# Attention by pairs of heads: shared loads, products on column halves, and the first block turned on TensorE

## The chip, the cores and the metric

One core of one Trainium2 chip. The metric is device microseconds of one execution. The kernel before ran three times: 1150.33, 1153.37 and 1156.15 us, median 1153.37 us. A profile is one further execution, with its own time.

## What is computed

Sparse attention over 4 batches x 8 heads x 576 rows x 64 columns, then two MLPs on the 2304 x 512 result. Per row of scores, only what lies within tau of the row's maximum is kept.

```python
scores = scale * np.matmul(q, k.transpose(0, 1, 3, 2))
thresh = np.max(scores, axis=-1, keepdims=True) - tau
scores = np.where(scores >= thresh, scores, -1000000000.0)
attn = np.exp(scores - np.max(scores, axis=-1, keepdims=True))
attn = attn / (np.sum(attn, axis=-1, keepdims=True) + 1e-09)
x = np.matmul(attn, v)                       # heads side by side: 2304 x 512
h = x @ w_in                                 # 512 -> 2048
x = (np.maximum(h, 0) + alpha * np.minimum(h, 0)) @ w_out
h = x @ w2_in
out = (h - np.tanh(h)) @ w2_out
```

The weights come as 64-bit words and are made into float32 on the chip.

## The kernel before

The 2304 rows are nine blocks of 256: block 2b and 2b+1 are the first and second 256 rows of batch b, and block 8 is the last 64 rows of all four batches. Attention fills the blocks in this order, and layer 1 of the MLP takes each block when its eight heads are there; layer 2 follows.

**Attention.** A visit is one head and one block (64 visits, eight to a block). `prep` (L461) loads the queries (`rq`, one half of the rows on each half of the partitions), the keys (`ks`, the same 64 rows on both halves) and `v` (`vs`), and splits v into three bfloat16 planes (`rest`, L490, on VectorE or GpSimd). `attend` (L600) makes the scores of two tiles of 128 rows, in float32 (L609): the two tiles lie on the two row halves of the array. `softmax` (L512) then does for each tile: a row maximum on VectorE (L524), a threshold (L527), a Prelu and an Exp on ScalarE (L287 as called from L530, and L534), the inverse of the sum (L537, L540), the normalised rows as float16 (`upper`, L542, on ScalarE, VectorE or GpSimd), their remainder as float16 (`lower`, L552, VectorE), a copy of 64 columns (`mend`, L554), and a transposing DMA from SyncE's queue into `eT` (`turn`, L561; 144 of them). The products (L620 to L626) are nine matmuls with 128 stationary columns (two planes of v side by side) and five with 64 (the third plane, on alternating column halves, the last with 64 rows). `x_copy` and `x_add` (L633, L638) add the two halves of the output into `xt`, and each second visit `x_hi` and `x_lo` split it for the MLP. After each second visit of an odd block, `attend_left` (L667) does the last 64 rows of two heads as one tile, with products at L688 to L692.

**PSUM.** Three score tiles `sc` of two banks: visits of block 0 (`FRONT`, `SOLO` = 8) use all three, one tile per step; later the third is `acc` of the MLP. One bank each is left for `hp` and `pt`.

**MLP.** Float32r with a high and a low part: L763 makes h in 24 matmuls of 256 columns per pair of column blocks, L950 the output of layer 1, L872 and L879 that of layer 2. 32 pieces of layer-1 weights (`piece`, L359) are loaded (512 KB each) and split during attention.

**Order.** Nothing runs by a fixed loop: each step is given to `Plan` (L74) with its engines, costs, a rank and what it reads and writes; the planner simulates engines and picks, for each engine, the ready step of the lowest rank. Its order is then each engine's program. The ranks are those of the visit (`TA` per tile) plus an offset of the kind of step (`OFF`), with `PREP` for the loads of attention and `PA`, `PB` for the weight pieces. `BUFS` says how many buffers a kind of tile has: two of `eT`, each for one visit. 140 dummy steps of two matmuls (`N_WARM`, L994 to L1000) take the lowest rank on TensorE.

```python
    for _ in range(N_WARM):
        add({"PE": 0.236}, 1e9, warm, [("const", 2)], [("hp", 0)], [("hp", 0)])
```

Of the kernel before, what the change touches and what calls it, by code (L numbers as in the profile page):

```python
# [7 lines left out]

F32 = mybir.dt.float32
# [14 lines left out]
P = 128  # L24
# [35 lines left out]
XR = -995.8426  # L60
FLEX = 1
T_WARM = 0.3
N_WARM = 140
DVE_PEN = 0.6331
OFF = {"S": -2993.86, "M": -246.5, "TH": -1456.02, "E": -819.06, "X": -255.04, "R": -398.47, "N": -1092.63, "NL": -1335.92, "F": -898.27, "DT": -1391.78, "AV": 1778.6, "XC": -777.36, "XH": 1070.62}
# [3 lines left out]
    "rq": 2, "ql": 1, "ks": 3, "vs": 3, "v3": 3, "e": 3, "st": 2, "eT": 2, "xt": 1, "rw": 4, "raw0": 2, "raw1": 3, "tw": 2,  # L69
    "x0": 2, "x1": 2, "mr": 1, "pair": 1, "xl": 1, "g": GB, "gs": 1, "o": 2,  # L70
# [160 lines left out]
def attention_mlp_mlp(ctx: ExitStack, tc: tile.TileContext, kv, q0, q1, tau, w1i, w1o, alpha, w2i, w2o, out):  # L231
# [23 lines left out]
    none = cpool.tile([P, P], F32, name="none")  # L255
    qscale = cpool.tile([P, 1], F32, name="qscale")
# [8 lines left out]
    sc = [ppool.tile([P, 1024], F32, name=f"sc{k}") for k in range(3)]  # L265
    acc = [sc[2][:, t * 512:(t + 1) * 512] for t in range(2)]
# [52 lines left out]
    def turned_float(l, kind, qd, c, rank):  # L319
# [33 lines left out]
        add({"LOAD": P * 4096 / DMA_RATE}, rank, load, reads=[("products", NV - 1), ("products", -NV)] * l, writes=[raw, (*raw, 0)], takes=[("rw", raw), (f"raw{l}", raw)], lag=DMA_LAG)  # L353
# [104 lines left out]
    def ends(v):  # L458
        return visits[v][1] and visits[v][2] % 2 == 0

    def prep(v, rank):  # L461
        b, qb, h = visits[v]
        k = brings[v]
        rq, ql, ks, vs = ("rq", v), ("ql", v), ("ks", k), ("vs", k)
        head_now[b, h] = k
# [19 lines left out]
        def load_v(e):
            x = take(tpool, vs, [P, 5, 2, D], F32, "vs", BUFS["vs"])
            e.dma_start(out=x[:, :, 0], in_=kv[b, h][:, KW:].rearrange("p (c d) -> p c d", c=5))


        def rest(e, n):  # L490
            x = T[vs]
            out_ = x[:, :, 1] if not n else take(tpool, ("v3", k), [P, 5, D], BF16, "v3", BUFS["v3"])
            e.tensor_tensor(out=out_, in0=x[:, :, n], in1=x.bitcast(BF16)[:, :, n, 1::2], op=ALU.subtract)

        add({"LOAD": rate * P}, rank - 6, load_q, [ROOM], [rq], takes=[("rq", rq)], lag=DMA_LAG)
        if k == v:
            add({"LOAD": rate * KW}, rank - 6, load_k, [ROOM], [ks], takes=[("ks", ks)], lag=DMA_LAG)
            add({"LOAD": rate * VW}, rank - 6, load_v, [ROOM], [(*vs, 0)], takes=[("vs", vs)], lag=DMA_LAG)
        if ends(v):
            add({"LOAD": rate * D}, rank - 6, load_left, [ROOM], [ql], takes=[("ql", ql)], lag=DMA_LAG)  # L500
        for key in (rq, ql) if ends(v) else (rq,):
            add({"ACT": 0.25}, rank, lambda e, key=key: scale(e, key), [("const", 0), ROOM], [key])
# [6 lines left out]
    def banks_of(s):  # L509
        return [("acc", t) for t in range(2)] if s == 2 else [("sc", s, t) for t in range(2)]  # L510

    def softmax(tile, n, slots, rank, alone=False):  # L512
# [5 lines left out]
        eT = ("eT", tile)  # L518
# [22 lines left out]

        def upper(e, j):  # L542
# [29 lines left out]
        for j, s in enumerate(slots):  # L572
            both = banks_of(s)
# [3 lines left out]
            add({"ACT": 0.72}, rank + OFF["X"], lambda e, j=j: row_exp(e, j), [("const", 0), ROOM], [(*ej, 0), (*st, 2, j)])  # L577
# [3 lines left out]
        for j in js:  # L581
# [4 lines left out]
            add({"ACT": 0.18, "POOL": 0.2}, rank + OFF["F"], lambda e, j=j: mend(e, j), [(*fj, 1), ROOM], [(*fj, 2)])  # L586
            k = add({"SYNC": 1.4}, rank + OFF["DT"], lambda e, j=j: turn(e, j), [*[(*fj, n_) for n_ in range(3)], ROOM], [(*eT, j)],
                    takes=[] if j else [("eT", eT)], lag=2.0, after=[k] if j else [])
        return [(*eT, j) for j in js]

    def planes(k, c):
        return T["vs", k].rearrange("p c a d -> p c (a d)").bitcast(BF16)[:, c, 1::2]

    def third(k, c, rows=slice(0, P)):
        return T["v3", k][rows, c]

    def with_v(k):
        return [("vs", k, 0), ("vs", k, 1), ("v3", k)]

    def attend(v, rank):  # L600
        b, qb, h = visits[v]
        k = head_now[b, h]

        slots = [(2 * v + j) % 3 for j in range(2)] if v < FRONT else (0, 1)

        def scores(e, js):
            for c in CHUNKS:
                for j in js:
                    e.matmul(  # L609
                        sc[slots[j]][:, 192:192 + S][:, c], lhsT=T["rq", v][HALVES[j]], rhs=T["ks", k][HALVES[j], c], start=True, stop=True,  # L610
                    )

        alone = v < SOLO
        for js in ((0,), (1,)) if alone else ((0, 1),):
            add({"PE": 1.3}, rank + OFF["S"], lambda e, js=js: scores(e, js), [("ks", k), ("rq", v), ROOM], [("sc", slots[j], "s") for j in js],
                [b_ for j in js for b_ in banks_of(slots[j])])
        reads = softmax(v, 2, slots, rank, alone)
        pk, po, bank = out_of(v)

        def products(e):  # L620
            eT = T["eT", v]
            for n in range(9):
                e.matmul(po, lhsT=planes(k, n % 5 if n < 5 else n - 5), rhs=eT[:, n], start=(n == 0), stop=False, skip_group_check=True)  # L623
            for c in range(5):
                rows = slice(0, P) if c < 4 else HALVES[0]
                e.matmul(po[HALVES[c % 2]], lhsT=third(k, c, rows), rhs=eT[rows, c], start=False, stop=(c > 2), skip_group_check=True)  # L626

        add({"PE": 1.32}, rank + OFF["AV"], products, [*reads, *with_v(k), ROOM], [pk, ("products", v)], bank)
        m = 2 * b + qb
        xt = ("xt", v // 2)  # L630
        half = slice((h % 2) * D, (h % 2 + 1) * D)

        def x_copy(e):  # L633
# [352 lines left out]
    def clear(e):  # L986
        e.memset(none, 0.0)
# [126 lines left out]
```

## Time and profile before

| | |
|---|---|
| median of three runs | 1153.37 us |
| the profiled execution | 1156.52 us, of which its span 1154.7 us |
| TensorE busy | 1104.4 us (96%) |
| VectorE, ScalarE, GpSimd busy | 785.3, 661.2, 116.6 us |
| DMA | 123.13 MB, 107 GB/s over the span |
| mean granted TensorE clock | 0.984 |

The profiled execution is 3.15 us above the median of the runs; what is summed against the profile is corrected by that. In the profile PE is TensorE's matmuls, PEld its weight loads, DVE VectorE, ACT ScalarE, POOL GpSimd and SP SyncE, whose queue issues the DMAs. Matmuls overlap, so the mean of one (some 280 ns) is longer than the distance from one to the next; a timeline shows that distance.

### The profile page before, as it was taken

To read this page: it belongs to the slowest core of one execution; us is meant where nothing else is said; L and a number is where in the kernel's file an instruction comes from. 1 tells how busy PE (TensorE), PEld (TensorE's weight loads), DVE (VectorE), ACT (ScalarE), POOL (GpSimd) and SP (SyncE) were. 2 spreads that over 40 slices of the span, in tenths; PEclk is the share of its full clock that TensorE was granted. 3 is DMA by queue.
4 is the path that set the end of the run, shared out by engine and by line. 5 is a ranking of instruction groups with operands and counts; after the bars stand their busy time and mean duration, and the time that the engine had idled before them with its cause. 6 is when DMAs were issued, how large, how long until landed. Compare 5 with 4: busy or idle time off the path is not lost. (4 is left out here: it accounts for less than half of the span.)

```text
span 1154.7 us, 22609 instructions
## 1 busy us (share of the span) xinstructions
PE 1104.4 (96%) x8670; PEld 979.2 (85%) x8670; DVE 785.3 (68%) x1693; ACT 661.2 (57%) x1371; POOL 116.6 (10%) x125
## 2 busy tenths in 40 slices
PE   8888999999999999899999999999999999999998
PEld 5556777887787787778778999999999999999997
DVE  6788797776677667767766554998556556566554
ACT  5787788778777767677776343763323323323222
POOL 0112322101111101010010000000000000000000
PEclk8899899999999999999999999999999999999999
DMA  7989898747677556674657231641010010010000
GB/s 205 217 189 180 182 224 174 156 92 149 132 144 146 103 128 140 137 142 99 133 99 182 92 110 49 205 150 44 13 37 19 19 37 11 28 37 11 10 19 19
DMA packets 248588, 123.13 MB, mean 107 GB/s; under 512 B 219040, under 2 KB 227232, under 8 KB 248480
## 3 DMA queue, kind: packets, MB, share of 16 engines
q1 hardware_dynamic: 248480, 121.69, 46.1%
q8 instruction: 68, 1.11, 0.4%
q14 instruction: 40, 0.33, 0.1%
HBM read 69.21 MB, written 9.96 MB: 69 GB/s over the span
## 5 line engine op out<-in xcount | busy, mean ns | idle before, releaser
L763 PE MATMUL hp<-x,ihi 128*128 128x256 f32 x1728 | 324.5, 287 | 1.7 <-DVE st L537 1.3
L763 PEld LDWEIGHTS hp<-x,ihi 128*128 128x128 f32 x1728 | 269.7, 192 | 15.3 <-issue 8.8
L763 PE MATMUL hp<-x,ilo 128*128 128x256 f32 x864 | 244.9, 283 | 0.0
L950 PE MATMUL sc<-g,ohi 128*128 128x256 f32 x1152 | 216.8, 287 | 1.1 <-ACT o L282 0.8
L950 PEld LDWEIGHTS sc<-g,ohi 128*128 128x128 f32 x1152 | 178.8, 191 | 12.1 <-issue 8.7
L763 PEld LDWEIGHTS hp<-x,ilo 128*128 128x128 f32 x864 | 166.2, 192 | 0.0
L950 PE MATMUL sc<-g,olo 128*128 128x256 f32 x576 | 162.7, 283 | 0.0
L872 PE MATMUL sc<-wp,g 128*128 128x256 f32 x1134 | 144.9, 283 | 0.0
L872 PEld LDWEIGHTS sc<-wp,g 128*128 128x128 f32 x1134 | 140.0, 192 | 0.0
L552 DVE SCALAR_TENSOR_TENSOR rw<-e,st,rw 128x576 f16<-128x576 f32 x144 | 118.8, 846 | 13.7 <-ACT rw L282 11.6
L524 DVE TENSOR_REDUCE st<-sc 128x1 f32<-128x576 f32 x144 | 105.9, 748 | 12.3 <-PE sc L609 8.4
L287 ACT ACTIVATE e<-sc,st 128x576 f32<-128x576 f32 x144 | 103.0, 735 | 14.7 <-DVE st L527 11.7
L534 ACT ACTIVATE e<-e,natau 128x576 f32<-128x576 f32 x144 | 110.3, 769 | 0.2
L950 PEld LDWEIGHTS sc<-g,olo 128*128 128x128 f32 x576 | 110.3, 191 | 0.0
L282 ACT ACTIVATE rw<-e,st 128x576 f16<-128x576 f32 x116 | 86.8, 768 | 37.9 <-issue 17.4
L282 ACT ACTIVATE g<-mr 128x512 fp32r<-128x512 f32 (+1 forms) x126 | 73.7, 585 | 56.8 <-DVE mr L782 39.2
L623 PE MATMUL pt<-eT,vs 128*128 128x256 f16 x576 | 78.2, 284 | 29.0 <-DMA eT<-rw 23.5
L763 PE MATMUL pt<-x,ihi 128*128 128x256 f32 x576 | 105.2, 283 | 0.0
L784 DVE SCALAR_TENSOR_TENSOR mr<-mr,nalpha,hp 128x256 f32<-128x256 f32 x144 | 62.7, 476 | 58.2 <-ACT mr L777 57.6
L609 PE MATMUL sc<-ks,rq 64*128 64x320 f32 (+1 forms) x512 | 89.0, 437 | 8.0 <-ACT rq L282 4.7
L290 DVE TENSOR_TENSOR g<-mr,g 128x512 fp32r<-128x512 f32 (+1 forms) x132 | 85.4, 647 | 16.4 <-ACT g L282 15.2
L623 PEld LDWEIGHTS <-vs 128*128 128x128 bf16 x576 | 53.4, 101 | 48.0 <-issue 31.8
(96 smaller groups left out, 1530.0 us busy)
## 6 DMA issues: line engine op xcount, KB each, us to landing
ks<-in_kv_dram SPq DMA_DIRECT2D x56, 288.0 KB, 3.3
vs<-in_kv_dram SPq DMA_DIRECT2D x56, 160.0 KB, 3.0
rw<-in_w1i_dram SPq DMA_DIRECT2D x16, 512.0 KB, 5.2
rw<-in_w1o_dram SPq DMA_DIRECT2D x16, 512.0 KB, 4.2
rw<-in_w2i_dram SPq DMA_DIRECT2D x16, 512.0 KB, 4.9
rw<-in_w2o_dram SPq DMA_DIRECT2D x16, 512.0 KB, 4.1
x1d<-o SPq DMA_DIRECT2D x18, 256.0 KB, 2.4
rw<-x1d SPq DMA_DIRECT2D x9, 512.0 KB, 3.6
```

The lines of the kernel that those rows point to most:

```text
L282: e.activation(out=out_, in_=in_, func=AF.Copy, **({} if scale is None else {"scale": scale}))
L287: e.activation(out=out_, in_=in_, func=AF.Prelu, alpha=alpha, **kw)
L290: e.tensor_tensor(out=out_, in0=in_, in1=hi.bitcast(F32), op=ALU.subtract)
L524: e.tensor_reduce(out=T[st][:, 0, j:j + 1], in_=x(s), axis=AX.X, op=ALU.max, negate=True)
L534: e.activation(out=w_, in_=w_, func=AF.Exp, bias=natau, scale=1.0, accum_out=T[st][:, 2, j:j + 1])
L552: e.scalar_tensor_tensor(out=x_[:, S + D:], in0=w_, scalar=r, in1=x_[:, :S], op0=ALU.mult, op1=ALU.subtract)
L609: e.matmul(sc[slots[j]][:, 192:192 + S][:, c], lhsT=T["rq", v][HALVES[j]], rhs=T["ks", k][HALVES[j], c], start=True, stop=True,)
L623: e.matmul(po, lhsT=planes(k, n % 5 if n < 5 else n - 5), rhs=eT[:, n], start=(n == 0), stop=False, skip_group_check=True)
L763: e.matmul(hq[:, k, :], lhsT=weight(l, "i", part, f // 4)[:, c, (f % 4) * P:(f % 4 + 1) * P], rhs=T[f"x{x}", m][:, c, :], start=(n0 + n == ...
L784: e.scalar_tensor_tensor(out=T[r][:, k, :], in0=T[r][:, k, :], scalar=nalpha[:, f0 + k:f0 + k + 1], in1=hq[:, k, :], op0=ALU.mult, op1=ALU ...
L872: e.matmul(out_, lhsT=x[:, a], rhs=y[:, b], start=(n == 0 and i == 0 and number in (1, 2, 5, 4)), stop=(n == NPAIR - 1 and i == 2), skip_g ...
L950: e.matmul(acc[t][:, (c % 2) * BLK:(c % 2 + 1) * BLK], lhsT=w[:, c * P:(c + 1) * P], rhs=g[:, k, :], start=(f == 0 and n == 0 and c % 2 == ...
```

## The change

Two visits in a row are now the two 128-row halves of one pair of heads. A visit's two score tiles are the two heads (not two halves of the rows of one head), and queries, keys and v come once for both visits of a pair: `q` is one tile for two heads with 256 or 320 columns (the last 64 rows included, so `ql` is gone), `ks` holds one head on each half of the partitions. The products of a pair are made once, after its second visit: 23 terms (three planes), each of them two matmuls with 64 stationary columns, one head on each column half. The output is then already in the MLP's layout: `x_copy`, `x_add` and `xt` are gone, for the left rows `pair` and its sum as well.

In the first four pairs (`WHOLE` = 4: block 0) the normalised rows stay float32, are transposed by matmuls against an identity (`turn_whole`, `turn_last`), copied to `eT` (`bring`, `bring_last`), and multiplied with v in float32; there v isn't split, and pair 4, which shares its heads with pair 3, loads its v again. `sc` has two tiles everywhere, `acc` its own two banks, `SOLO` is 0; `eT` has three buffers of one head and 256 rows; 110 dummy steps; the planner's ranks are other ones.

```diff
-TA = 13.1642
-PA, PB = 81.361, 4.1836
-PREP = 63.9042
-FRONT, SOLO = 8, 8
+TA = 3.0306
+PA, PB = 1607.411, 3.1322
+PREP = 2618.4454
+WHOLE, SOLO = 4, 0
-N_WARM = 140
+N_WARM = 110
-    "rq": 2, "ql": 1, "ks": 3, "vs": 3, "v3": 3, "e": 3, "st": 2, "eT": 2, "xt": 1, "rw": 4, "raw0": 2, "raw1": 3, "tw": 2,
+    "q": 2, "ks": 2, "vs": 4, "v3": 3, "e": 3, "st": 2, "eT": 3, "rw": 4, "raw0": 2, "raw1": 3, "tw": 2,
-    sc = [ppool.tile([P, 1024], F32, name=f"sc{k}") for k in range(3)]
-    acc = [sc[2][:, t * 512:(t + 1) * 512] for t in range(2)]
+    sc = [ppool.tile([P, 1024], F32, name=f"sc{k}") for k in range(2)]
+    acc = [ppool.tile([P, 512], F32, name=f"acc{t}") for t in range(2)]
...
         def load_q(e):
-            x = take(tpool, rq, [P, P], F32, "rq", BUFS["rq"])
+            x = take(tpool, q, [P, BLK + D], F32, "q", BUFS["q"])
             for a in range(2):
-                e.dma_start(out=x[HALVES[a]], in_=packed_q[qb][b, h][HALVES[a], a * P:(a + 1) * P])
+                e.dma_start(out=x[HALVES[a], :width], in_=packed_q[qb][b, h + a][HALVES[a]])
...
+        def load_k(e):
+            x = take(tpool, ks, [P, S], F32, "ks", BUFS["ks"])
             for a in range(2):
+                e.dma_start(out=x[HALVES[a]], in_=kv[b, h + a][HALVES[a], :S])
...
+        def turn_whole(e, j):
+            x_ = T["e", (tile, j)]
+            for c in range(4):
+                e.transpose(pt[:, c, :], x_[:, c * P:(c + 1) * P], ident)
+
+        def turn_last(e, j):
+            e.transpose(hp[:D, j, :P], T["e", (tile, j)][:, 4 * P:], ident)
+
+        def bring(e, j):
+            key, at, _ = eT[j]
+            if not at:
+                take(tpool, key, [P, 9 * P], F32, "eT", BUFS["eT"])
+            copy(e, T[key][:, :8 * P].rearrange("p (c q) -> p c q", c=4)[:, :, at * P:(at + 1) * P], pt)
...
+    TERMS = [(part, i, i if i < 5 else i - 5) for i in range(9) for part in range(2)] + [(2, i, i) for i in range(5)]
+
+    def summed(e, po, k, eT):
+        for i, (part, block, c) in enumerate(TERMS):
+            for a in range(2):
+                e.matmul(po[HALVES[a]], lhsT=plane((k, a), part, c), rhs=eT(a, block), start=(i == 0), stop=(i == len(TERMS) - 1), skip_group_check=True)
...
+        softmax(v, 2, slots, rank, [(("eT", (u, a)), j, 2) for a in range(2)], alone, one(u))
+        if j:
+            attended(u, rank)
...
         def x_hi(e):
...
+            copy(e, T["x0", m][:, c, :], po, scale=1 / UNIT)
 
         def x_lo(e):
-            sub(e, T["x1", m][:, h // 2, :], T[xt], T["x0", m][:, h // 2, :])
+            e.scalar_tensor_tensor(out=T["x1", m][:, c, :], in0=po, scalar=1 / UNIT, in1=T["x0", m][:, c, :].bitcast(F32), op0=ALU.mult, op1=ALU.subtract)
```

## Rows read from the trace of the kernel before

**Rows 1.** The page, part 1: busy time and its share of the span.
```profile
PE 1104.4 (96%) x8670; PEld 979.2 (85%) x8670; DVE 785.3 (68%) x1693; ACT 661.2 (57%) x1371; POOL 116.6 (10%) x125
```

**Rows 2.** Windows by stage: stretch, length, busy time of each engine, clock, DMA share, GB/s.
```profile
0.00:88.60 88.60, 72.96 (x473) 49.11 (x473) 65.30 (x144) 63.23 (x135) 11.58 (x19) 0.88 0.87 201
88.60:175.00 86.40, 77.39 (x583) 61.45 (x583) 72.96 (x150) 69.36 (x150) 27.45 (x29) 0.93 0.92 197
175.00:630.00 455.00, 434.83 (x3492) 358.91 (x3491) 322.59 (x718) 340.87 (x768) 56.01 (x68) 1.00 0.65 133
630.00:1154.70 524.70, 519.18 (x4129) 509.75 (x4128) 324.49 (x682) 187.75 (x319) 21.59 (x10) 1.00 0.16 53
```

**Rows 3.** Groups of lines, PE by shape, 0 to 88.6 us: the dummy matmuls.
```profile
L996 PE MATMUL hp<-none 128*128 128x256 bf16 x280 | 38.8, 303 | 1.0 <-POOL none L987 1.0
```

**Rows 4.** Timeline of PE, 84 to 93 us: layer 1's first matmul.
```profile
88.59 0.79 PE L763 MATMUL hp<-x,ihi 128*128 128x256 f32 x2
```

**Rows 5.** Timeline of PE, 304.4 to 307.6 us: one visit's products, one visit's scores.
```profile
304.40 1.14 PE L623 MATMUL pt<-eT,vs 128*128 128x256 f16 x9 [0.55 <-DMA eT<-rw]
305.47 0.63 PE L626 MATMUL pt<-eT,v 128*64 128x256 f16 x5
306.03 1.24 PE L609 MATMUL sc<-ks,rq 64*128 64x320 f32 x8
```

**Rows 6.** The same timeline cut to 305.40 to 305.62 us, PE and then PEld.
```profile
305.16 0.38 PE L623 MATMUL pt<-eT,vs 128*128 128x256 f16 x2
...
305.27 0.27 PE L623 MATMUL pt<-eT,vs 128*128 128x256 f16 x1
305.47 0.41 PE L626 MATMUL pt<-eT,v 128*64 128x256 f16 x4
...
305.47 0.14 PEld L626 LDWEIGHTS <-v 128*64 128x64 bf16 x4 [0.21 <-issue]
```

**Rows 7.** Timeline of PE, 308.4 to 310.2 us: products of the left rows.
```profile
308.73 0.40 PE L688 MATMUL pt<-eT,vs 128*128 128x128 f16 x4
...
310.09 0.39 PE L950 MATMUL sc<-g,ohi 128*128 128x256 f32 x1
```

**Rows 8.** Groups of lines by shape, ACT and DVE: busy us, mean ns.
```profile
L287 ACT ACTIVATE e<-sc,st 128x576 f32<-128x576 f32 x144 | 103.0, 735 | 14.7 <-DVE st L527 11.7 <-DVE st L540 1.0 <-DVE st L537 0.6
...
L282 ACT ACTIVATE rw<-rw 128x64 f16<-128x64 f16 x142 | 34.4, 249 | 12.1 <-DVE rw L552 11.6
...
L282 ACT ACTIVATE xt<-pt 64x256 f32<-64x256 f32 x64 | 24.3, 380 | 16.9 <-PE pt L626 15.4
...
L282 ACT ACTIVATE o<-sc 128x512 f32<-128x512 f32 x18 | 10.3, 594 | 5.1 <-PE sc L950 5.0
...
L282 ACT ACTIVATE pair<-pt 64x128 f32<-64x128 f32 x32 | 8.7, 272 | 3.1 <-PE pt L692 1.5 <-POOL xl L709 0.8 <-DVE xt L639 0.4
...
L552 DVE SCALAR_TENSOR_TENSOR rw<-e,st,rw 128x576 f16<-128x576 f32 x144 | 118.8, 846 | 13.7 <-ACT rw L282 11.6 <-DMA rq<-in_q_dram 1.5
L524 DVE TENSOR_REDUCE st<-sc 128x1 f32<-128x576 f32 x144 | 105.9, 748 | 12.3 <-PE sc L609 8.4 <-PE sc L675 3.3
...
L639 DVE SCALAR_TENSOR_TENSOR xt<-pt,xt 64x256 f32<-64x256 f32 x64 | 26.6, 416 | 30.9 <-ACT xt L282 30.0
...
L493 DVE TENSOR_TENSOR v<-vs 128x320 bf16<-128x320 f32 x39 | 19.3, 498 | 4.0 <-POOL vs L493 3.7
```

**Rows 9.** DMA view of 225 to 250 us: the queue's share of 16 engines; transposes, us to landing.
```profile
q1 hardware_dynamic: 8887, 2.29, 46.7%
...
eT<-rw SPq DMA_TRANSPOSE x6, 3.3
```

**Rows 10.** Line L561: its issues, ns min/median/max, first and last start.
```profile
L561 SPq DMA_TRANSPOSE eT<-rw x144: 1242/1318/2921, 17.0 to 619.6; - x144
```

**Rows 11.** Waits: who waited for whom, us in total, times, longest.
```profile
PE pt L623 <- DMA eT<-rw: 23.5, 22, 3.2
```

**Rows 12.** The chain that ended last: the end of layer 1's matmuls.
```profile
758.99 2.88 PE sc L950 x24
```

More of the change, by code (lines that the diff above doesn't have):

```diff
@@ L443, in attention_mlp_mlp @@
     for b in range(B):
-        for qb, order in ((0, range(H)), (1, reversed(range(H)))):
+        for qb, order in ((0, range(0, H, 2)), (1, range(H - 2, -1, -2))):
             for h in order:
-                visits.append((b, qb, h))
-                unit.append(n_unit)
-                n_unit += 3 if qb and h % 2 == 0 else 2
+                for j in range(2):
+                    visits.append((b, qb, h))
+                    unit.append(n_unit)
+                    n_unit += 3 if qb and j else 2
@@ L449, in attention_mlp_mlp @@
     NV = len(visits)
     brings = []
-    for v in range(NV):
-        brings.append(next((brings[w] for w in range(max(0, v - 3), v) if visits[w][::2] == visits[v][::2]), v))
-    head_now = {}
+    for u in range(NV // 2):
+        same = u and visits[2 * u][::2] == visits[2 * u - 1][::2]
+        brings.append(brings[u - 1] if same else u)
+    brings_v = [brings[u] if u != WHOLE else u for u in range(NV // 2)]
     begun = {}
     HALVES = (slice(0, D), slice(D, P))
-    def ends(v):
-        return visits[v][1] and visits[v][2] % 2 == 0
@@ L485, in load_v @@
[L485 to L502, printed above, removed]
@@ L507, in attention_mlp_mlp, with softmax @@
     CHUNKS = (slice(0, 320), slice(320, S))
-    def banks_of(s):
-        return [("acc", t) for t in range(2)] if s == 2 else [("sc", s, t) for t in range(2)]
-    def softmax(tile, n, slots, rank, alone=False):
+    def softmax(tile, n, slots, rank, eT, alone=False, w=False):
         def x(s):
@@ L572, in softmax @@
         for j, s in enumerate(slots):
-            both = banks_of(s)
+            both = [("sc", s, t) for t in range(2)]
             ej = ("e", (tile, j))
@@ L585, in softmax @@
             add({"DVE": 0.73}, rank + OFF["NL"], lambda e, j=j: lower(e, j), [(*ej, 0), (*st, 3), (*fj, 0), ROOM], [(*fj, 1)])
[L586 to L598, printed above, removed]
+            add({"ACT": 0.15, "POOL": 0.19}, rank + OFF["F"], lambda e, j=j: mend(e, j), [(*fj, 1), ROOM], [(*fj, 2)])
+            key, at, _ = eT[j]
+            begun[key] = add({"SYNC": 1.37}, rank + OFF["DT"], lambda e, j=j: turn(e, j), [*[(*fj, n_) for n_ in range(3)], ROOM], [(*key, at)],
+                takes=[] if at else [("eT", key)], lag=2.0, after=[begun[key]] if at else [])
@@ L611, in scores @@
                     )
         alone = v < SOLO
[L614 to L618, printed above, removed]
-        def products(e):
[L621 to L633, printed above, removed]
-            if v % 2 == 0:
-                take(tpool, xt, [P, BLK], F32, "xt", BUFS["xt"])
-            copy(e, T[xt][half], po[D:P], scale=1 / UNIT)
-        def x_add(e):
-            e.scalar_tensor_tensor(out=T[xt][half], in0=po[:D], scalar=1 / UNIT, in1=T[xt][half], op0=ALU.mult, op1=ALU.add)
+        for heads in ((0,), (1,)) if alone else ((0, 1),):
+            add({"PE": 1.3}, rank + OFF["S"], lambda e, heads=heads: scores(e, heads), [("ks", k), ("q", u), ROOM], [("sc", slots[a], "s") for a in heads],
+                [b_ for a in heads for b_ in (("sc", slots[a], 0), ("sc", slots[a], 1))])
@@ new lines, in attend, with attended @@
+        softmax(v, 2, slots, rank, [(("eT", (u, a)), j, 2) for a in range(2)], alone, one(u))
+        if j:
+            attended(u, rank)
+    def attended(u, rank):
+        b, qb, h = visits[2 * u]
+        k, w = brings_v[u], one(u)
+        pk, po, bank = out_of(u)
+        def products(e):
+            eT = [T["eT", (u, a)] for a in range(2)]
+            if not w:
+                summed(e, po, k, lambda a, block: eT[a][:, block])
+                return
+            for c in range(4):
+                for a in range(2):
+                    e.matmul(po[HALVES[a]], lhsT=T["vs", (k, a)][:, 0, c], rhs=eT[a][:, c * BLK:(c + 1) * BLK], start=(c == 0), stop=False, skip_group_check=True)
+            for j in range(2):
+                for a in range(2):
+                    e.matmul(po[HALVES[a], j * P:(j + 1) * P], lhsT=T["vs", (k, a)][HALVES[a], 0, 4], rhs=eT[j][HALVES[a], 8 * P:],
+                             start=False, stop=True, skip_group_check=True)
+        reads = [("eT", (u, a), *x) for a in range(2) for x in ([(0,), (1,)] + [(5, 0), (5, 1)] * w)]
+        add({"PE": 2.3 if w else 2.7}, rank + OFF["AV"], products, [*reads, *with_v(k, w), ROOM], [pk, ("products", u)], bank)
+        m, c = 2 * b + qb, h // 2
@@ L653, in attend @@
-        add({"DVE": 0.4}, rank + OFF["XC"], x_add, [pk, ROOM], [xk], bank)
-        if v % 2:
-            takes = [(f"x{part}", (f"x{part}", m)) for part in range(2)] if v % H == 1 else []
-            begun[m] = add(any_of(0.31, 0.2, 0.37), rank + OFF["XH"], x_hi, [(*xt, 0), (*xt, 1), ROOM], [("x0", m, h // 2)],
-                           takes=takes, after=[begun[m]] if m in begun else [])
-            add(either(0.34, 0.69), rank + OFF["XH"], x_lo, [(*xt, 0), (*xt, 1), ("x0", m, h // 2), ROOM], [("x1", m, h // 2)])
+            e.scalar_tensor_tensor(out=T["x1", m][:, c, :], in0=po, scalar=1 / UNIT, in1=T["x0", m][:, c, :].bitcast(F32), op0=ALU.mult, op1=ALU.subtract)
@@ L660, in attention_mlp_mlp, with out_of @@
+        takes = [] if u % 4 else [(f"x{part}", (f"x{part}", m)) for part in range(2)]
+        begun[m] = add({"ACT": 0.3}, rank + OFF["XC"], x_hi, [pk, ROOM], [("x0", m, c)], bank, takes=takes, after=[begun[m]] if m in begun else [])
+        add({"DVE": 0.39}, rank + OFF["XC"], x_lo, [pk, ("x0", m, c), ROOM], [("x1", m, c)], bank)
     n_out = [0]
-    def out_of(v):
+    def out_of(u):
+        if 0 <= u < WHOLE:
+            return ("acc", ("po", u % 2)), acc[0][:, u % 2 * BLK:][:, :BLK], [("acc", 0)]
@@ L715, in attend_left, with x_copy @@
-        add({"SYNC": 0.3}, rank + OFF["XC"], lambda e: e.dma_start(out=x8d[:, h // 2, b, :], in_=T[xl]), [ROOM, (*xl, 0), (*xl, 1)], [("x8d", 0, b, h)], lag=3.0)
+            eT = T[eT_]
+            summed(e, po[:, :D], kv_, lambda a, block: eT[:, block, a * D:(a + 1) * D])
+        add({"PE": 1.5}, rank + OFF["AV"], products, [(*eT_, 0), *with_v(kv_), ROOM], [pk, ("products", -u - 1)], bank)
+        xl = ("xl", u)
+        def x_copy(e):
+            copy(e, take(tpool, xl, [P, D], F32, "xl", BUFS["xl"]), po[:, :D], scale=1 / UNIT)
@@ L720, in load_x @@
+        add({"ACT": 0.2}, rank + OFF["XC"], x_copy, [pk, ROOM], [xl], bank, takes=[("xl", xl)])
+        add({"SYNC": 0.6}, rank + OFF["XC"], lambda e: e.dma_start(out=x8d[:, h // 2, b, :], in_=T[xl]), [ROOM, xl], [("x8d", 0, b, h)], lag=3.0)
     def load_x(m, rank):
```

192 lines of the change are left out of this document (103 added, 89 removed).

## The prediction

> **What bounds the kernel now.** The page's first part comes first: TensorE is busy for 96% of the span, VectorE for 68% [rows 1]. So I look for where TensorE's time isn't real work. The windows by stage [rows 2] show four stages. After 630 us TensorE is full; the change touches nothing there. From 175 to 630 us it is busy for 434.8 of 455 us at clock 1.00: only less work on TensorE, or its 20 idle us, can give time. Before 88.6 us layer 1 hasn't begun: its first matmul is at 88.59 [rows 4], and of the 73.0 us busy 38.8 are dummies [rows 3], so 88.6 - (73.0 - 38.8) = 54 us carry no work. What ends late there is not TensorE: the DMA engines are 87% busy and still 92% up to 175 us, while ScalarE and VectorE have a quarter free [rows 2]. The early stage is held by DMA and by the chain through it; everything later by TensorE.
>
> **Block 0.** Removed per tile of block 0: `lower` 0.846 and `mend` 0.249 [rows 8], the transposing DMA, and its place in SyncE's queue (1.3 us an issue [rows 10]). `normalise` costs what `upper` did. Added: `bring`, nearest row the 128x512 copy out of PSUM at 0.594, and `bring_last`, nearest the 64x128 copy at 0.272 [rows 8]. Over 16 tiles -17.5 + 13.9. The v splits go: 16 x 0.50 = -8.0; `x_copy` and `x_add`, 2 x (0.380 + 0.416) a pair, four pairs: -6.4 [rows 8]; fewer, wider scalings, at most -1.5. The three engines held 63.2 + 65.3 + 11.6 = 140.1 us up to 88.6 [rows 2]; -19.5 leaves 120.6. How long that takes hangs on how many engines work at once: 140.1 / 88.6 = 1.58 up to 88.6 us, (73.0 + 69.4 + 27.5) / 86.4 = 1.97 after it [rows 2]. At 1.58 layer 1 begins at 76 us, at 1.97 at 61 us. I take 1.77, the middle, because the DMA relief lifts the fill but the chain per tile stays: **68 us, 20.6 us saved**.
>
> The relief: between 225 and 250 us the queue was 46.7% busy with six transposes and little else, 11.7 us or under 2.0 us a transpose [rows 9]; 16 fewer take 31 us of 16 engines. Keys come once instead of twice, half of 56 loads, q in half as many issues: a bonus I leave uncounted. Against it: the weight pieces now rank ahead of attention's first loads, so the first scores start later by two loads of 512 KB, some 5 us at 201 GB/s [rows 2]; it is inside the 61 to 76.
>
> TensorE in block 0: eight scores of 1.24 [rows 5]; the transposes have no row. As plain float32 they cost at most what the scores do, 1.24 us for 576 columns in a row pair, 640 columns being 1.4 us a tile; at least what layer 1's matmuls do, 2.88 / 24 = 0.12 for 256 columns [rows 12], 0.3 a tile. I take the upper end, the type being that of the scores. The float32 products, 4 x 256 + 2 x 128 columns in column pairs, are 2.8 us a pair. Together 9.9 + 22.4 + 11.2 = 43.5 us, below 68 and covered by the time TensorE has free. Two score tiles instead of three: a visit's loop is 1.24 + 2 x 0.748 + 2 x 0.735 = 4.2 us [rows 5, 8], five with threshold and hand-overs, 40 for eight: below 68 too. The dummies, the identity on GpSimd and the second load of pair 4's v (320 KB) fill idle places; if the cover went they'd cost 26, 1 and 2 us.
>
> **Products of the other 28 pairs.** Two visits cost 2 x (306.03 - 304.40) = 3.26 us [rows 5]. That is more than its matmuls: they follow at 0.11 (305.16 to 305.27) and the first with 64 columns comes 0.20 after the last with 128 [rows 6], so a change of array shape costs 0.09, and each visit has three. Now all 46 have one shape. Four of them with their loads are over in 0.41 us where one lasts 0.27 to 0.30, and four loads take 0.14 [rows 6]: the halves run side by side. In a long chain nothing shows them: a pair of matmuls at least the 0.11 of its stream, at most 0.41 - 0.28 = 0.13, the distance of the two pairs seen. I take 0.11, since that 0.13 holds the first, uncovered load. 23 x 0.11 + 0.03 + two changes 0.19 = 2.75. Saved 0.51 x 28 = **14.3 us** (range 1 to 15).
>
> **Left rows.** 16 times 310.09 - 308.73 = 1.36 [rows 7] becomes 23 pairs of 64 columns at 0.03 to 0.06 plus 0.2; at 0.045 it is 1.24: **1.9 us** saved (range -4 to 7).
>
> **Waits.** TensorE waited 23.5 us in 22 waits for `eT` [rows 11], about one product group in four; groups fall from 80 to 48, but each waits for four tiles. I take **3.5 us**, between 0 and 9. Savings on ScalarE and VectorE after block 0 I cost at nothing: both have 25% or more free [rows 2].
>
> **Sum.** 1156.5 - 20.6 - 14.3 - 1.9 - 3.5 = 1116.2; the profiled run lay 3.1 above the median of 1153.4, so **1113 us**.
>
> **Rivals.** *The early stage doesn't get shorter* (0.14). Layer 1 begins sooner but waits for its weight pieces, which need VectorE and ScalarE as before; for it speaks the fill of 1.97 right after 88.6 us, where little room is left. 1113 + 20.6 = 1134.
>
> *The early stage gains more* (0.12). If DMA alone sets it, 31 us of transposes and 6 of keys go from a stage 87 to 92% busy: 41 us instead of 20.6, so 1093. Against it: the three engines then need a fill of over two.
>
> *Each column pair waits for its loads* (0.10): 0.134 and 0.06 as in the one step seen. 28 x 23 x 0.024 + 16 x 23 x 0.015 = 21: 1134.
>
> *The left rows are held by their weight loads* (0.05). Should two loads for the halves run one after the other and take as long as a 256-column stream, 0.11, a left group takes 2.7, 1.5 more: 16 x 1.5 = 23, 1136; the pairs' products don't change. Rows 6 speak against it: four loads in 0.14. The Trainium skill has the rule: "TensorEngine Tiling (Array Packing)", Restrictions, says that column tiling switches fast weight load off, and "TensorE: Matmul & The Clock Gate", LDWEIGHTS, gives columns over 1.2 GHz, 53 ns for 64 columns, which for two in a row makes this case, an estimate from that page; the loads of rows 6 go faster.
>
> *Slower: `eT` stalls* (0.07). A pair holds two of three `eT` buffers until its products, so the second tile after a pair's end can't be turned before, and SyncE's queue stands behind it, loads too. 144 tiles in 17.0 to 619.6 us [rows 10] are one in 4.2 us, so there are 8.4 us for landing 3.3 [rows 9], products 2.75, and each group of layer 1 put ahead, 2.88 [rows 12]. With one ahead it costs 0.5, with three 6.3 us a pair: 27 x 6.3 = 170. TensorE fills it with layer 1 for a while: layer 1 ends at 761.87 [rows 12], some 135 us after the last transpose has landed and been used; 46 of them (384 matmuls of 0.12) are block 8, which can't start earlier. So 89 are absorbed: 1113 + 170 - 89 = 1194. It decides from (89 + 40) / 27 = 4.8 us a pair. Against it: the order is planned with these times, and one group ahead is the usual.
>
> *The halves don't run side by side* (0.05), so that the change doesn't do what it says: 28 x 23 x 0.11 + 16 x 23 x 0.045 = 87: 1200. Rows 6 speak against it.
>
> Two of the smaller losses with no gain early make no change (0.04).
>
> **Numbers.** The forecast has 0.43 and its own range is 1100 to 1126. Faster are it and the first four rivals, 0.84; the same 0.04 (0.5% or 6 us is about what a measurement tells from none); slower 0.12. The range of 1088 to 1142 takes in those four and the bounds of the unknown costs, and leaves out the slower cases and the best of the gain.
>
> **What would show it.** Layer 1's first matmul near 68 us and DMA share below 0.8 before it; the products as 46 matmuls in some 2.7 us, 0.11 from pair to pair; left groups near 1.2; idle TensorE from 175 us to attention's end not above 20 us. Wrong: a first layer-1 matmul after 80 us, a product group over 3.2 us, or waits of the transposes for `eT` of several us a pair.

## The result, and the profile after

The kernel after took **1083.66 us** (1083.33 to 1086.65, four runs) against 1153.82 of the kernel before in the same comparison, a ratio of 0.940 with a 95% interval of 0.937 to 0.943. The forecast was 1113 us, 1088 to 1142: the direction was right, the gain of 70 us lay beyond the range. The profiled execution has a span of 1081.5 us instead of 1154.7.

The page's first part, which answers to [rows 1]:

```profile
PE 1058.8 (98%) x9594; PEld 979.0 (91%) x9594; DVE 768.2 (71%) x1638; ACT 569.5 (53%) x1135; POOL 124.1 (11%) x142
```

Windows of the kernel after, with the columns of [rows 2]: to the first layer-1 matmul, to 150 us, to the end of attention, and the rest.

```profile
0.00:69.17 69.17, 61.71 (x476) 45.18 (x476) 57.02 (x128) 49.23 (x96) 26.39 (x37) 0.98 0.63 188
69.17:150.00 80.83, 75.14 (x773) 66.29 (x772) 73.21 (x152) 62.50 (x133) 20.29 (x21) 0.96 0.88 200
150.00:553.00 403.00, 399.05 (x4192) 354.00 (x4191) 306.41 (x663) 276.00 (x597) 54.99 (x73) 1.00 0.67 132
553.00:1081.50 528.50, 522.89 (x4161) 513.49 (x4159) 331.57 (x697) 181.72 (x311) 22.42 (x11) 1.00 0.17 54
```

Before the first layer-1 matmul the DMA engines are 63% busy instead of 87%, and the three other engines work 57.0 + 49.2 + 26.4 us in 69.2, a fill of 1.92. In the third stage TensorE idles for 4 of 403 us instead of 20 of 455. The last stage is as long as it was, within 4 us.

Timeline of PE after, the end of block 0 (answers to [rows 4]), a pair's products at 308.59 (to [rows 5]) and a left group at 236.10 (to [rows 7]); start, length, line:

```profile
68.59 0.65 PE L677 MATMUL acc<-eT,vs 64*64 64x128 f32 x8
69.17 0.51 PE L782 MATMUL hp<-x,ihi 128*128 128x256 f32 x2
...
308.59 2.16 PE L637 MATMUL pt<-eT,vs 128*64 128x256 f16 x36
310.58 0.71 PE L637 MATMUL pt<-eT,v 128*64 128x256 f16 x10
311.23 0.50 PE L782 MATMUL hp<-x,ihi 128*128 128x256 f32 x2
...
236.10 0.77 PE L637 MATMUL pt<-eT,vs 128*64 128x64 f16 x36
236.69 0.33 PE L637 MATMUL pt<-eT,v 128*64 128x64 f16 x10
236.95 0.50 PE L969 MATMUL acc<-g,ohi 128*128 128x256 f32 x2
```

46 matmuls of 256 columns take 311.23 - 308.59 = 2.64 us, those of 64 columns 236.95 - 236.10 = 0.85. TensorE's waits after, longest first (columns as in [rows 11]):

```profile
PE pt L637 <- DMA eT<-rw: 3.6, 6, 0.9
PE pt L551 <- ACT e L284: 3.5, 3, 2.7
PE pt L551 <- DVE eT L286: 2.5, 3, 1.0
PE hp L782 <- DVE st L539: 2.2, 1, 2.2
```

Before, behind the first layer-1 matmul alone (the other 9.1 us of [rows 11] lie in block 0):

```profile
PE pt L623 <- DMA eT<-rw: 14.4, 16, 2.5
```

So the products wait 3.6 us for `eT`, where in the same stretch they waited 14.4.

**Where 73.2 us of span went.** In both traces I summed the distance from each matmul to the next, by kind, behind the first layer-1 matmul, with what exceeds 0.45 us counted as a wait; the first 0.45 us stay with the matmul's kind. "Two clocks, old ranks" is experiment e7 below.

| us of span | before | after | difference | forecast | e7: two clocks, old ranks |
|---|---|---|---|---|---|
| up to the first layer-1 matmul | 88.6 | 69.2 | -19.4 | -20.6 | 71.2 |
| products, pairs and left rows | 116.9 | 89.6 | -27.3 | -16.2 | 94.3 |
| waits of TensorE over 0.45 us | 24.6 | 8.0 | -16.6 | -3.5 | 21.7 |
| scores | 87.0 | 82.2 | -4.8 | 0 | 88.7 |
| the two MLPs | 833.0 | 827.7 | -5.3 | 0 | 830.2 |

The front came as forecast. The products gave 11 us more; the waits and the last two rows 23 us that the forecast didn't have. Of the 16.6 us of waits 12.9 fall in the third stage (15.3 before, 2.4 after) and 3.7 in the second.

The last two rows are waits too, for the most part. Of the distances over 0.45 us, 26 followed a matmul of the MLPs and 14 one of the scores; after, 5 and 2. At 0.45 us less a usual distance of 0.12 to 0.15, these 33 make some 10 us, and the two rows gain 10.1.

### The profile page after: what moved, and what is told of

The parts are those of the page before. It is cut to its first block, busy times and chain, and to the rows that moved or that the text cites. A ratio compares the mean times of both kernels' runs of the same rounds, so it can differ in the third digit from the quotient of the medians.

```text
span 1081.5 us, 23833 instructions
## 1 busy us (share of the span) xinstructions
PE 1058.8 (98%) x9594; PEld 979.0 (91%) x9594; DVE 768.2 (71%) x1638; ACT 569.5 (53%) x1135; POOL 124.1 (11%) x142
## 4 chain that ended last, share of the span: by engine, by line
PE 53%; DVE 1%; ACT 0%; issue 0%; DVEq 0%; ACTq 0%
PE hp L782 17%; PE sc L891 13%; PE pt L782 10%; PE acc L969 8%; PE sc L898 5%; PE pt L637 1%; PE sc L649 0%; PE sc L715 0%; ACT e L289 0%; DVE rw L575 0%; DVE st L523 0%; DVE o L924 0%; ACT e L533 0%; DVE rw L571 0%; DVE st L526 0%
## 5 line engine op out<-in xcount | busy, mean ns | idle before, releaser
L969 PE MATMUL acc<-g,ohi 128*128 128x256 f32 x1152 | 215.7, 287 | 0.0
L969 PEld LDWEIGHTS acc<-g,ohi 128*128 128x128 f32 x1152 | 179.3, 192 | 10.0 <-issue 9.4
L969 PE MATMUL acc<-g,olo 128*128 128x256 f32 x576 | 162.9, 283 | 0.0
L289 ACT ACTIVATE e<-sc,st 128x576 f32<-128x576 f32 x144 | 101.8, 737 | 26.4 <-DVE st L526 25.5
L969 PEld LDWEIGHTS acc<-g,olo 128*128 128x128 f32 x576 | 110.5, 192 | 0.0
L575 DVE SCALAR_TENSOR_TENSOR rw<-e,st,rw 128x576 f16<-128x576 f32 x128 | 104.2, 840 | 2.9 <-ACT rw L284 2.5
L782 PEld LDWEIGHTS pt<-x,ihi 128*128 128x128 f32 x576 | 90.9, 192 | 1.3
L649 PE MATMUL sc<-ks,q 64*128 64x320 f32 (+1 forms) x512 | 82.3, 433 | 1.1 <-ACT e L289 0.7
L796 ACT ACTIVATE mr<-hp 128x512 f32<-128x512 f32 x72 | 42.7, 593 | 76.0 <-PE hp L782 73.4
L782 PE MATMUL pt<-x,ilo 128*128 128x256 f32 x288 | 81.5, 283 | 0.0
L637 PE MATMUL pt<-eT,vs 128*64 128x256 f16 (+1 forms) x1584 | 74.3, 246 | 3.8 <-DMA eT<-rw 3.6
```

What stands on the lines that cost most here:

```text
L289: e.activation(out=out_, in_=in_, func=AF.Prelu, alpha=alpha, **kw)
L575: e.scalar_tensor_tensor(out=x_[:, S + D:], in0=w_, scalar=r, in1=x_[:, :S], op0=ALU.mult, op1=ALU.subtract)
L637: e.matmul(po[HALVES[a]], lhsT=plane((k, a), part, c), rhs=eT(a, block), start=(i == 0), stop=(i == len(TERMS) - 1), skip_group_check=True)
L649: e.matmul(sc[slots[a]][:, 192:192 + S][:, c], lhsT=T["q", u][HALVES[a], j * P:(j + 1) * P], rhs=T["ks", k][HALVES[a], c], start=True, sto ...
L782: e.matmul(hq[:, k, :], lhsT=weight(l, "i", part, f // 4)[:, c, (f % 4) * P:(f % 4 + 1) * P], rhs=T[f"x{x}", m][:, c, :], start=(n0 + n == ...
L969: e.matmul(acc[t][:, (c % 2) * BLK:(c % 2 + 1) * BLK], lhsT=w[:, c * P:(c + 1) * P], rhs=g[:, k, :], start=(f == 0 and n == 0 and c % 2 == ...
```

## The experiments

All are compared with the kernel before by ratio; 0.01 of it is 11.5 us. The kernel after stands at 0.940 or 1083.7 us. Differences in us are those of the medians; taken from the ratios, those against the kernel after come out 1 to 3 us larger, since the kernel before ran at 1149 to 1151 us beside the experiments and at 1153.8 beside the kernel after.

### One part of the planner: how many clocks SyncE's queue has

The change has a part that the description above and the forecast passed over: before, the planner counted loads on a clock of their own, LOAD, though they are issued by the same queue as the transposes and stores (SYNC). After, one clock counts all.

**e3.** The five loads again on LOAD:

```diff
-LAG = {..., "SYNC": 0.0}
+LAG = {..., "SYNC": 0.0, "LOAD": 0.0}
-        add({"SYNC": max(1.1, rate * width)}, rank - 6, load_q, ...
+        add({"LOAD": max(1.1, rate * width)}, rank - 6, load_q, ...
```

> The kernel after, but the planner again counts SyncE's loads on a clock of their own (LOAD), beside that of the transposes and stores, as in the kernel before. Theory (TensorE's waits went from 24.6 to 8.0 us behind the first layer-1 matmul because the planner now knows that loads and transposes stand in one queue): waits of 18 us or more, most of them of the products for eT, time 1094 to 1102 us. Rival (they went because a product group comes once for a pair, or by the ranks): waits below 12 us, time 1080 to 1089 us.

Measured: **1110.1 us**, ratio 0.964 (0.961 to 0.968), 26 us slower; the waits are 22.7 us. The longest waits of TensorE in e3's profile:

```profile
PE pt L637 <- DMA eT<-rw: 13.3, 17, 1.9
PE sc L649 <- ACT e L289: 6.0, 6, 2.9
PE hp L782 <- DVE mr L803: 4.1, 4, 2.4
```

17 waits and 13.3 us of the products for `eT`, where the kernel after has 6 and 3.6: the theory holds, and the loss is beyond its 1102 us. Scores, products and MLPs lose 4.6, 7.4 and 5.0 us more, in part as the first 0.45 us of waits.

**e4.** The old ranks and penalties, one clock.

```diff
-TA = 3.0306
+TA = 13.1642
...
-OFF = {"S": -1656.89, "M": -1361.12, ...}
+OFF = {"S": -2993.86, "M": -246.5, ..., "T": -1391.78, "H": -777.36, ...}
```

> The kernel after with the planner's ranks and penalties of the kernel before (TA to OFF; transposes on TensorE ranked as the DMA's were, their copies as the copies of x were); buffers, dummies and steps as in the kernel after. Theory (the ranks are what took TensorE's waits away): waits of 18 us or more, time 1095 to 1110 us. Rival (the steps themselves did): waits below 12 us behind the first layer-1 matmul, time 1082 to 1092 us.

Measured: **1093.5 us**, 0.951 (0.948 to 0.953), 10 us slower, waits 14.4. Between the two: the ranks are worth 10 us, a third of the planner's part.

**e7.** Both undone.

```diff
-        add({"SYNC": max(1.1, rate * width)}, rank - 6, load_q, ...
+        add({"LOAD": max(1.1, rate * width)}, rank - 6, load_q, ...
-TA = 3.0306
+TA = 13.1642
...
```

> The kernel after with both: two clocks for SyncE's queue and the ranks of the kernel before. So all of the planner's part is undone and all steps are kept. With one clock and these ranks it took 1093 us. Theory (two clocks cost by themselves, whatever the ranks): 1108 to 1125 us, waits of 20 us or more. Rival (the 26 us of two clocks were a mismatch with the new ranks): 1088 to 1098 us, waits near 14 us.

Measured: **1114.7 us**, 0.970 (0.966 to 0.973), waits 21.7. Two clocks cost 21 us under the old ranks and 26 under the new: it is no mismatch. And this kernel, all steps of the change under the planner of before, is what the forecast described: 1113. That it comes so near is partly luck: by the table its products gave 22.6 us instead of 16.2, its front 17.4 instead of 20.6.

**e5, e6.** The kernel before with one clock, and with one clock and the new ranks.

```diff
-        add({"LOAD": rate * P}, rank - 6, load_q, ...
+        add({"SYNC": rate * P}, rank - 6, load_q, ...
```

> The kernel before, with one change: the planner counts the loads on the clock of SyncE's transposes and stores (LOAD becomes SYNC). No step, buffer or rank changes. Theory (two clocks for one queue put loads in front of transposes that TensorE then waits for; in the kernel after, going back to two clocks cost 26 us): the waits behind the first layer-1 matmul fall from 24.6 us to 12 or less, time 1130 to 1142 us against 1150. Rival (the cost of two clocks in the kernel after is a mismatch with ranks made for one, and the same holds here the other way round): 1150 us or slower.

> The kernel before, with one clock for SyncE's queue and with the ranks and penalties of the kernel after: all of the change that lies in the planner, none of its steps. Theory (the planner's part is worth some 25 us, the steps the other 45): 1120 to 1135 us, waits behind the first layer-1 matmul below 12 us. Rival (the ranks fit only the new steps): 1145 us or slower.

Measured: e5 **1140.3 us**, 0.991 (0.987 to 0.994); e6 **1147.4 us**, 0.997 (0.995 to 0.999). The products' waits for `eT` in e5, block 0 included, fall by half against [rows 11]:

```profile
PE pt L623 <- DMA eT<-rw: 11.8, 8, 5.7
```

but all waits behind the first layer-1 matmul only from 24.6 to 18.7 us, not to 12, and the 25th layer-1 matmul comes at 106.6 us instead of 98.4; the gain is 10 us. In e6 it comes at 118.4, with waits of 27.8 us: the new ranks don't fit the old steps, so the rival holds there and my sum of 25 + 45 fell. The planner's part is worth 31 us on the new steps (e7 to after) and 3 to 10 on the old.

**e11.** A control: another order without another step.

```diff
-        add({"PE": 1.5}, rank + OFF["AV"], products, ...
+        add({"PE": 0.9}, rank + OFF["AV"], products, ...
```

> The kernel after, the planner told 0.9 us (as measured) instead of 1.5 us for a left group's products; no step changes, only the order. A measure of what a slightly different order is worth by itself. Theory (the order is near its best, one cost in sixty groups doesn't matter): 1080 to 1088 us. Rival (each reshuffle moves the time by as much as two clocks did): 1095 us or more.

Measured: **1085.8 us**, 0.944 (0.942 to 0.946). One small reshuffle moved the time by 2 us, not by 10 or 26.

### The column halves

**e1.**

```diff
-        for i, (part, block, c) in enumerate(TERMS):
-            for a in range(2):
+        for a in range(2):
+            for i, (part, block, c) in enumerate(TERMS):
```

> The kernel after, but the 46 matmuls of a pair's products are issued as 23 of one head and then 23 of the other, so that no two neighbours lie on different column halves. Theory (the halves run side by side, and TensorE sets the time): a pair's group goes from 2.70 us to 46 x 0.109 + 0.2 = 5.2 us, 28 x 2.5 = 70 us; a left group from 0.87 us to 46 x 0.03 to 0.056, 1.4 to 2.6 us, 8 to 28 us more; 1084 + 78 to 98 = 1162 to 1182 us. Rival (the saving comes from one shape instead of three, not from the halves side by side): the groups stay near 2.7 us and the time within 5 us of 1084.

Measured: **1138.3 us**, 0.990 (0.987 to 0.992), 55 us slower. The pairs' products went from 75.7 to 130.2 us, 4.65 a pair, the left groups from 13.9 to 23.4. The halves side by side are shown, and that TensorE sets the time: 54.5 + 9.5 us more of products gave 55 us of time, and the rest came back in shorter waits (3.2 us instead of 8.0) and MLPs (3.6 us less). Below the expected 1162, since even here a few matmuls overlap where one head follows the other. Timeline of PE in e1; `v` is the third plane, the last five terms of a head, `vs` the first:

```profile
308.02 2.15 PE L637 MATMUL pt<-eT,vs 128*64 128x256 f16 x18
310.01 0.38 PE L637 MATMUL pt<-eT,v 128*64 128x256 f16 x2
310.13 0.30 PE L637 MATMUL pt<-eT,vs 128*64 128x256 f16 x1
310.23 0.27 PE L637 MATMUL pt<-eT,v 128*64 128x256 f16 x1
310.26 0.27 PE L637 MATMUL pt<-eT,vs 128*64 128x256 f16 x1
310.34 0.27 PE L637 MATMUL pt<-eT,v 128*64 128x256 f16 x1
310.37 0.27 PE L637 MATMUL pt<-eT,vs 128*64 128x256 f16 x1
310.45 0.27 PE L637 MATMUL pt<-eT,v 128*64 128x256 f16 x1
```

The second head's first matmul starts at 310.13, before the first head's last three at 310.23, 310.34 and 310.45, though it stands behind them in the program.

**e8.** Products after each visit, 128 columns.

```diff
-        if j:
-            attended(u, rank)
+        if j or not one(u):
+            attended(u, rank, j)
...
+                at = slice(half * P, (half + 1) * P)
+                summed(e, po[:, at], k, lambda a, block: eT[a][:, block, at])
```

> The kernel after, but outside block 0 the products are made after each visit, over 128 columns, so 56 groups instead of 28, each waiting for its own two tiles as in the kernel before. On TensorE a group is 23 pairs at 0.056 plus 0.2, 1.5 us; two of them 3.0 instead of 2.7: 28 x 0.3 = 8 us. Theory (waits went because groups are half as many): waits behind the first layer-1 matmul rise from 8.0 by 8 or more besides, 1098 to 1106 us. Rival (the number of groups doesn't matter where the order is right): waits within 4 us of 8.0, 1088 to 1095 us.

Measured: **1098.9 us**, 0.955 (0.953 to 0.958), 15 us slower; products 97.8 instead of 89.6, as expected; waits 11.1 instead of 8.0. By waits the rival holds: twice as many groups cost 3 us of them. The time lies in the theory's range: besides 8 us of products and 3 of waits, the front took 1.3 us more, the scores 1.0 and the MLPs 2.2.

### Block 0

**e2, e9.** Block 0 by the transposing DMA, under the new ranks (e2) and the old (e9, against e4).

```diff
-WHOLE, SOLO = 4, 0
+WHOLE, SOLO = 0, 0
```

> The kernel after with WHOLE = 0: block 0's tiles are split and turned by the transposing DMA like all others, its products are the 23 float16 terms. Theory (turning on TensorE is what brought layer 1's first matmul from 88.6 to 69.2 us, by taking 16 transposes off the DMA engines): the first layer-1 matmul at 84 to 90 us, time 1099 to 1106 us. Rival (the front got shorter because there are fewer steps on ScalarE and VectorE, one load per pair, and other ranks): first layer-1 matmul before 77 us, time 1084 to 1092 us.

> The kernel after with the ranks of the kernel before (1093 us as such) and with block 0 by the transposing DMA. Theory (turning block 0 on TensorE is worth some 29 us whatever the ranks, as it was with the new ones): 1114 to 1128 us. Rival (those 29 us were ranks made for the other block 0): 1093 to 1103 us.

Measured: e2 **1113.1 us**, 0.968 (0.966 to 0.970), 29 us slower and 7 beyond the theory's range; e9 **1110.2 us**, 0.965 (0.963 to 0.967), 17 us slower than e4 and between the two expectations. Here the mark I had named misleads: the first six layer-1 matmuls come at 54.5 us, as soon as the first pairs are there, but the 25th only at 108.2 instead of 77.8. e2's windows, with the columns of [rows 2]:

```profile
0.00:54.50 54.50, 46.10 (x360) 35.74 (x360) 43.87 (x97) 35.85 (x73) 5.35 (x12) 0.87 0.82 213
54.50:108.20 53.70, 25.25 (x166) 18.04 (x165) 45.57 (x95) 33.23 (x69) 6.11 (x8) 0.68 0.89 213
```

Its longest waits of TensorE:

```profile
PE sc L649 <- ACT e L289: 17.3, 6, 4.8
PE sc L649 <- DMA ks<-in_kv_dram: 14.2, 1, 14.2
```

DMA is at 82 and 89% again, and the scores wait 14.2 us for one load of keys. That load is issued at 65.19 us, behind four transposes and four weight loads in SyncE's queue (from 52.78 us on), and the scores start at 70.26. So turning block 0 on TensorE is worth 17 to 29 us. How much of that is the DMA engines, how much the queue and how much other work isn't shown, as the edit brings `lower`, `mend` and the v splits back together with the transposes. (e2 also lacks the third score tile that the kernel before had in its front.)

**e12.** Block 0's heads one at a time.

```diff
-WHOLE, SOLO = 4, 0
+WHOLE, SOLO = 4, 8
```

> The kernel after with SOLO = 8: block 0's scores and thresholds one head at a time, as in the kernel before (with two score tiles, not three). Theory (the loop through two score tiles is below what the other engines need in block 0): first layer-1 matmul within 3 us of 69, time 1081 to 1088 us. Rival (a visit's loop sets block 0): first layer-1 matmul 4 to 10 us sooner, as one head's scores needn't wait for both tiles, 1074 to 1080 us.

Measured: **1083.1 us**, 0.942 (0.940 to 0.943), first layer-1 matmul at 70.5 us. The same as the kernel after; the loop through two score tiles is not the bound.

### The copies that went

**e10, e13, e14.** The old path's two copies and two adds a pair put back between `x_hi` and `x_lo`, in all pairs, in pairs 8 to 31, in pairs 0 to 3. They write where `x_lo` then writes.

```diff
+        for a in range(2):
+            add({"ACT": 0.4}, rank + OFF["XC"], lambda e, a=a: x_copy(e, a), [pk, ("x0", m, c), ROOM], [("x1", m, c)], bank)
+            add({"DVE": 0.4}, rank + OFF["XC"], lambda e, a=a: x_add(e, a), [pk, ROOM], [("x1", m, c)], bank)
         add({"DVE": 0.39}, rank + OFF["XC"], x_lo, ...
```

> The kernel after with the work of the old output path put back beside the new one: for each pair two more 64x256 copies on ScalarE and two more 64x256 adds on VectorE, between x_hi and x_lo, 0.76 and 0.83 us a pair. Theory (the copies saved after block 0 are worth nothing, since TensorE sets the time there): 1083 to 1089 us. Rival (ScalarE and VectorE set the pace, and their relief is where the unforeseen gain came from): 32 x 0.8 = 26 us, 1100 to 1112 us.

> As e10 (two copies and two adds more a pair, which cost 16 us over 32 pairs), but only in pairs 8 to 31, from block 2 on. Theory (ScalarE and VectorE are short only until the layer-1 weights are split, some 165 us; later the copies cost nothing): 1082 to 1087 us. Rival (the copies cost all the way, by their share 24 / 32 of 16 us): 1093 to 1098 us.

> As e10, but only in pairs 0 to 3, block 0. Theory (nearly all of the 16 us is lost between block 0 and the last weight piece): 1088 to 1098 us, the 25th layer-1 matmul at 84 us or later instead of 77.8. Rival (they cost by their share, 4 / 32): 1084 to 1087 us.

Measured: e10 **1099.8 us**, 0.956 (0.955 to 0.958); e13 **1087.2 us**, 0.945 (0.942 to 0.948); e14 **1102.2 us**, 0.958 (0.955 to 0.960). e10 lies at the rival's edge; e13 and e14 say why: four pairs of block 0 cost all of it, 18 us, 24 later pairs 4. It isn't the 6 us of work but the chain. In the kernel after, block 0's last products end at 69.17; ScalarE's `x_hi` and VectorE's `x_lo` of that pair:

```profile
69.73 0.38 ACT L284 ACTIVATE x<-acc 128x256 fp32r<-128x256 f32 x1
...
70.37 0.41 DVE L691 SCALAR_TENSOR_TENSOR x<-acc,x 128x256 fp32r<-128x256 f32 x1
```

In e14 they end at 71.11, and the chain is (ACT and DVE timelines, then PE's):

```profile
71.26 0.39 ACT L284 ACTIVATE x<-acc 128x256 fp32r<-128x256 f32 x1 [1.17 <-PE acc L677]
...
73.34 0.38 ACT L284 ACTIVATE x<-acc 64x256 fp32r<-64x256 f32 x1
...
78.47 0.38 ACT L284 ACTIVATE x<-acc 64x256 fp32r<-64x256 f32 x1
...
73.98 0.41 DVE L700 SCALAR_TENSOR_TENSOR x<-acc,x 64x256 fp32r<-64x256 f32 x1
...
79.25 0.42 DVE L700 SCALAR_TENSOR_TENSOR x<-acc,x 64x256 fp32r<-64x256 f32 x1
...
81.16 0.42 DVE L691 SCALAR_TENSOR_TENSOR x<-acc,x 128x256 fp32r<-128x256 f32 x1
...
81.63 0.58 PE L792 MATMUL hp<-x,ihi 128*128 128x256 f32 x1 [3.52 <-DVE x L691]
```

Four more steps of 0.4 us made 10.5 us (71.11 to 81.58) out of 1.6 (69.17 to 70.78), as each stands behind other work of its engine; layer 1 goes on at 81.63, and its 25th matmul comes at 90.0 instead of 77.8.

This is not what the change saved. In e14 the four steps stand in a row behind the last products; in the kernel before only one copy and one add did, as the other head's products came a visit sooner. There the last products of block 0 end at 88.59 (ACT, DVE, POOL timelines; `x_copy`, `x_add`, `x_hi`, `x_lo`):

```profile
88.70 0.38 ACT L282 ACTIVATE xt<-pt 64x256 f32<-64x256 f32 x1 [1.38 <-PE pt L626]
...
89.11 0.42 DVE L639 SCALAR_TENSOR_TENSOR xt<-pt,xt 64x256 f32<-64x256 f32 x1 [1.11 <-ACT xt L282]
89.57 0.29 DVE L284 TENSOR_SCALAR x<-xt 128x256 fp32r<-128x256 f32 x1
...
89.94 1.10 POOL L290 TENSOR_TENSOR x<-xt,x 128x256 fp32r<-128x256 f32 x1 [3.93 <-DVE x L284]
```

That is 2.4 us (88.59 to 91.04) against 1.6. e14 shows what a longer chain at this place costs, and no gain of the change.

None of the fourteen is faster than the kernel after beyond the scatter of the runs.

## Why the prediction was wrong

**What failed** is the step from the steps to the order. The sum priced what is added and removed, and took the planner's order as given: "between 0 and 9" for TensorE's waits, nothing for the rest. That term was to fall by 3.5 us and fell by 16.6, or some 27 with the first 0.45 us of each wait. But the planner of the kernel before had been told that loads and transposes don't share a queue, and the change puts that right. The edit was in the diff; it stands in no term and no rival. Setting it and the ranks back gives 1114.7 us (e7), my number; setting both as in the kernel after gives 31 us more, 21 to 26 of them by the one clock (e3, e7 against e4), the rest by the ranks.

**Block 0** was right in its number: 20.6 us, measured 19.4. In part that is luck: the fill I took at 1.77 was 1.92, the work 132.6 instead of 120.6 us (GpSimd's went from 11.6 to 26.4), and the two errors cancel. The reason given, DMA, is supported by the DMA share (63% instead of 87%) and by e2 and e9, but not shown apart from the steps that went with the transposes; and the 2.0 us of 16 engines for a transpose was a bound from above: seven loads of 32 KB and two of 160 KB, a quarter of the bytes, lie in the same 25 us. The transposes, costed at their upper end of 1.4 us a tile, took 0.66 (19.87 to 20.53 in the trace), under half of the scores' price for a column (TensorE waited 6.0 us ahead of them, in a place that it had free). "Savings on ScalarE and VectorE after block 0 I cost at nothing" holds from block 2 on within 4 us (e13). The shorter chain at the end of block 0 wasn't costed, and it gave little: from the first to the 25th layer-1 matmul there are 9.8 us before (88.6 to 98.4) and 8.6 after (69.2 to 77.8). The first layer-1 matmul was the wrong mark all the same (e2), though here both marks came forward alike, by 19.4 and 20.6 us.

**Products of the pairs**: the mechanism was right (e1), 0.109 from pair to pair and 2.64 to 2.70 against the 2.75 forecast. Mis-sized was the side of before: I took one visit, 1.63; all 56 took 95.1 us, 1.70 each. Saved 19.4 instead of 14.3.

**Left rows** were mis-sized: 13.9 / 16 = 0.87 instead of 1.24, since the pairs of 64 columns follow at the lower bound of 0.03. Saved 7.9 instead of 1.9. With it the rival of the loads of 0.11 fell: 23 pairs in 0.85 us leave 0.037 for two loads of 64 columns. The Trainium skill, "TensorE: Matmul & The Clock Gate", LDWEIGHTS, gives columns over 1.2 GHz for a load, an estimate of 53 ns for 64 columns and 0.107 us for two in a row. Two in a row are not seen here; the measurement decides.

**Waits**: besides the order, the reading was off. Of the 23.5 us of [rows 11] 9.1 lie in block 0, whose time another term already held; 14.4 were left to save behind it, and 10.8 of them went.

**The rivals**: `eT` stalls (slower) cost little: behind 69 us the transposes waited 15.5 us in 8 waits for the products to free `eT`, 0.6 us a pair where 4.8 would have decided, and the products' waits are 3.6 us. "Each column pair waits for its loads" fell with the 0.109. "The early stage gains more" did not come true: 19.4 us were gained at the first layer-1 matmul, 20.6 at the 25th, and 3.7 us of waits in the second stage behind it.

**Not settled**: what in the front is the DMA engines' share, and how the planner's 31 us would come out under other orders than these; of small reshuffles there is one (e11). TensorE's lower clock is no part of the gain in the MLPs: from one of their matmuls to the next there are in the second stage 0.128 us before and 0.133 after, gaps over 0.45 left out (granted clock 0.93 in the stage of [rows 2], 0.96 after, but 0.84 from 69 to 90 us).

## What to carry to other kernels

Where a planner writes the order, read its model in the diff before the steps: a resource that it counts twice is paid in waits, here 21 to 26 us on a kernel whose steps had saved 35. Price a step on the path by its place, too: four more steps of 0.4 us at a stage's end took 9 us behind other work, and the same steps later cost next to nothing. And mark a stage by the point from which it runs steadily, not by its first instruction.

## What the runs showed of the hardware

- Matmuls on different column halves start out of program order, by the starts in the trace: in e1 the second head's first matmul starts 0.32 us before the first head's last (310.13 and 310.45), and 46 of them take 4.65 us instead of the 5.2 estimated for a row of single matmuls (46 x 0.109 + 0.2).
- Two matmuls of 64 columns on the two halves (64 stationary columns each) with their two weight loads take 0.85 / 23 = 0.037 us, the change of shape included.
- A float32 transpose of 128 columns on TensorE takes some 0.11 us (0.44 for four, 19.87 to 20.31), under half of what the float32 scores need for as many columns of a row pair (1.17 us for 576, 16.72 to 17.89, so 0.26).
